# A gated recurrence and a soft mixture of experts on one Trainium2 core: seven experts' second layers summed in four row groups before one turn to 128 rows, and another order of the last partial sums

## The chip, the core and the metric

The kernel runs on one core of a Trainium2 chip. The metric is the device time of one execution in microseconds (us), and a kernel's figure is the median of several executions. The engines are TensorE (PE for its matmuls, PEld for its weight loads), VectorE (DVE), ScalarE (ACT), GpSimd (POOL) and SyncE (SP, which here only issues DMAs). Sixteen DMA engines move data between HBM and the core's SBUF; matmuls write to PSUM banks.

## What is computed

The input `x` is 4 batches x 5056 tokens x 256 channels. A gated recurrence runs over the tokens of each batch, and a soft mixture of experts follows on all 20224 rows of its output. Cut to what matters:

```python
f = lower_bound + (1 - lower_bound) * sigmoid(f_logit)
for t in range(S):
    h = f[:, t] * h + (1 - f[:, t]) * x[:, t]        # y[:, t] = h
logits = y @ phi                                     # 20224 x 32 slots (8 experts x 4)
d = softmax of logits over the rows                  # column by column
slot_input = d.T @ y                                 # 32 x 256
slot_out = per expert: relu(slot_input @ w1) @ w2    # w1 256 x 1024, w2 1024 x 256
out = (softmax of logits over the 32 slots) @ slot_out
```

The output is 20224 x 256 in float32.

## The kernel before, in words

The order of the instructions on every engine is the order of the code (a manual schedule): no planner moves them.

**Main loop (lines 479 to 566).** Forty units (10 token groups of 512 tokens x 4 batches) are loaded by SP, go through the sigmoid (ACT), the products (POOL), transposes (PE), the scan along the tokens (DVE), back to token order, and yield logits, their exponentials `etall` (slots on partitions, the four batches stacked as 4 x 32 = 128 rows) and the sum `slot_ps` of weighted rows. Meanwhile POOL issues the loads of the experts' weights (L135 to L147), w1 of all eight experts first, then w2. The tiles of the last two experts share one buffer, `w_t`; the last expert's tile comes in three parts of four, two and two of its eight chunks `fc`.

**Between loop and experts (L568 to L593).** POOL clears two tiles, `hid` (L571, 1024 columns of bf16) and `wide` (L572, 4096 columns). The last slot sums follow, and `spin` (L150) issues matmuls whose result nobody reads: six ahead of the copy of `slot_ps` (L584) and six behind the sum that makes the slot inputs (L593).

**The experts' first layer (L620 to L654).** For four experts at a time, `hi_ps` is computed in four strips of 32 output rows (L621); relu goes to `hi0` and `hi1`, and PE transposes them into `ht_ps`. Of a 32-column block only the expert's own four slots are wanted. For experts 0 to 3 they are copied into `hid` (L645, ACT), which is zero elsewhere, one 32-column block per expert and chunk. For experts 4 to 7 they are copied into `wide` (L653, twice ACT and twice DVE), repeated for the four batches, so a block has 128 columns.

**The second layer (L655 to L710).** This is where the change lies. Experts 0 to 3 use 128x32 matmuls: chunk `fc` goes to the row group `fc % 4` of the bank `so4_ps` (L658), so four matmuls can stand beside each other on the array, and the four row groups hold four partial sums of the 32 slots. DVE copies them to `so4` (L664), and one fp32 matmul with `rep2` (L719) adds the four groups and repeats the sum for the four batches: 128 rows, in the bank `so_ps`. Experts 4 to 7 use 128x128 matmuls (L705) that add the repeated rows directly to `so_ps`. Row sums of the exponentials (`row_sums`, L393) and four `spin` matmuls lie between the experts. The last expert's upper four chunks (`late`) go to another bank, `sb_ps`.

**The last sums (L688 to L736).** When the last expert's chunk 3 is summed, ACT makes `part_b` (L712, bf16) and DVE `part` (L713, fp32) from `so_ps`, both scaled. DVE's `slot_out` (L728) is `sb_ps` scaled plus `part`. For two rows of tokens the kernel goes around `slot_out`: `early_ps[r]` takes four matmuls with `gs`, which already holds the exponentials times the hidden values of the late chunks (`early_row`, L694), and one with `part_b` (`early_part`, L699). On PE the order is: late chunks 4 and 5, `early_row(0)` for them, `early_part(0)`, `early_part(1)`, late chunks 6 and 7, the other six of `early_row`. ACT scales both rows (L734, tile `early`) and SP stores each (L736). POOL makes `slot_bd` (L738, two instructions) from `slot_out`.

**The output stage (L741 to L845).** `pieces` (L774) makes the first block of the last batch: 32x256 matmuls from `slot_out` (`share`, L755) into PSUM banks `op`, evictions by DVE (L745) and ACT (L749) into two tiles `ob`, and a store by SP after every second or fourth row (L785). `couple` (L804) makes two batches at once from `slot_bd` (L811) into `oc`, stored at L817; `rest` (L834) and `whole` (L802) do what remains. The first two banks `op` are those that `early_ps` used.

Of the kernel before, what the change touches and what calls it, by code (L numbers as in the profile page):

```python
# [9 lines left out]
F32 = mybir.dt.float32  # L10
BF16 = mybir.dt.bfloat16
AX = mybir.AxisListType
ALU = mybir.AluOpType
ACT = mybir.ActivationFunctionType
# [4 lines left out]
def kernel(  # L19
# [10 lines left out]
    nc = tc.nc  # L30
    B, S, D = x.shape
    E = moe_w1.shape[0]
    F = moe_w1.shape[2]
    NS = moe_phi.shape[1]
    SPE = NS // E
    P = 128
    DC = D // P
    FC = F // P
    R = 4
    G = P * R  # L40
    n_grp = (S + G - 1) // G
# [18 lines left out]
    wide_r = 4 * R  # L60
# [60 lines left out]
    rrow = store.tile([P, n_grp * R, B], F32, name="rrow")  # L121
# [10 lines left out]
    w1_sb = [wts.tile([P, DC, F], BF16, name=f"w1_sb{e}") for e in range(E)]  # L132
    w2_sb = [wts.tile([P, FC, D], BF16, name=f"w2_sb{e}") for e in range(E - 2)]
# [16 lines left out]
    def spin(dst, k, w):  # L150
        for _ in range(k):
            nc.tensor.matmul(dst[:, ds(0, w)], w1_sb[0][:, 0, :P], w1_sb[0][:, 0, :w],
                             start=True, stop=True, skip_group_check=True)

    W_AT = {9: 1, 17: 1, 25: 1, 31: 1, 32: 1, 33: 2, 34: 3, 36: 6}
    w_next = [0]
# [4 lines left out]
    ld = held.enter_context(tc.tile_pool(name="ld", bufs=3))  # L161
    with tc.tile_pool(name="sp2", bufs=3) as sp2, \
# [316 lines left out]
        for n in range(n_unit):  # L479
# [82 lines left out]
            elif not n >= n_unit - 6:  # L562
# [2 lines left out]
                batch(slots, n - 4, 1)  # L565
                if n > 2 * B and n % (2 * B) == 3:
                    idle(1)
        hid, wide = (ld.tile([P, 2, R, D], F32, name=i, tag="x_t") for i in ("hid", "wide"))  # L568
        hid = hid.rearrange("p u r d -> p (u r d)").bitcast(BF16)[:, ds(0, FC * E // 2 * NS)]
        wide = wide.rearrange("p u r d -> p (u r d)").bitcast(BF16)[:, ds(0, FC * E // 2 * P)]  # L570
        nc.gpsimd.memset(hid, 0.0)  # L571
        nc.gpsimd.memset(wide, 0.0)  # L572
        hid = hid.rearrange("p (f e s) -> p f e s", f=FC, s=NS)
        wide = wide.rearrange("p (f w b s) -> p f w b s", f=FC, b=B, s=NS)
        logits(last, [3])
        late_exps()
        left_over()
# [3 lines left out]
        late_weights()  # L581
        slots(odd)
        late_slots()
        spin(tail[:, 1], 6, D)  # L584
        slot_sb = hpool.tile([P, G, DC], BF16, name="slot_sb", tag="h")
        slot_sb = slot_sb.rearrange("p t o -> p (t o)").bitcast(F32)[:, ds(0, D)]
        nc.vector.tensor_copy(slot_sb, slot_ps)
# [2 lines left out]
        for o in range(DC):  # L590
            nc.tensor.matmul(sin_ps[:, o], slot_v[:, o], rep[:, 0],
                             start=True, stop=True, skip_group_check=True)
        spin(slot_bank[:, 1], 6, D)  # L593

    with tc.tile_pool(name="ew", bufs=1) as ew, \
         tc.tile_pool(name="pm", bufs=2, space=PSUM) as pm, \
# [14 lines left out]
        Q = 4  # L611
# [20 lines left out]
        for q in range(E // Q):  # L632
            ht_ps = psu.tile([P, FC, P], BF16, name="ht_ps", tag="up")
            hi_v = his[q].rearrange("p (c f) -> p f c", f=FC)
            for fc in range(FC):
                nc.tensor.transpose(ht_ps[:, fc], hi_v[:, fc], ident)
            if q == 0:
                nc.tensor.matmul(cs_ps, rep2, cs1, start=True, stop=True)
                src = ht_ps.rearrange("p f (j s) -> p f j s", s=NS)[:, :, :, ds(0, SPE)]
                src = bass.AP(tensor=src.tensor, offset=src.offset,  # L640
                              ap=[list(src.ap[0]), [P, FC], [NS + SPE, Q], [1, SPE]])
                dst = hid[:, :, :, ds(0, SPE)]
                dst = bass.AP(tensor=dst.tensor, offset=dst.offset,
                              ap=[list(dst.ap[0]), [Q * NS, FC], [NS + SPE, Q], [1, SPE]])
                nc.scalar.copy(dst, src)  # L645
                nc.vector.reciprocal(rcs, cs_ps)
                nc.vector.tensor_tensor(of_last, of_last, rcs, ALU.mult)
                continue
            for j in range(Q):
                s0 = (Q + j) * SPE  # L650
                src = ht_ps[:, :, ds(j * NS + s0, SPE)]
                copy = nc.scalar.copy if j % 2 == 0 else nc.vector.tensor_copy
                copy(wide[:, :, j, :, ds(s0, SPE)],  # L653
                     src.unsqueeze(2).broadcast_to([P, FC, B, SPE]))  # L654
        so4_ps = pm.tile([P, D], F32, name="so4_ps", tag="pm")  # L655
        for e in range(Q):
            for fc in range(FC):
                nc.tensor.matmul(so4_ps[ds(fc % 4 * NS, NS), :], hid[:, fc, e],  # L658
                                 w2_sb[e][:, fc],
                                 start=(e == 0 and fc < 4),  # L660
                                 stop=(e == Q - 1 and fc >= FC - 4),
                                 skip_group_check=True)
        so4 = ew.tile([P, D], F32, name="so4")
        nc.vector.tensor_copy(so4, so4_ps)  # L664

        tail_b = ds((B - 1) * NS, NS)
        ex = ew.tile([P, 2, P], BF16, name="ex")
# [24 lines left out]
        def early_row(r, k, n):  # L692
            for i in range(k, k + n):
                nc.tensor.matmul(early_ps[r], gs[:, i, r], w2_sb[E - 1][:, FC - n_late + i],  # L694
                                 start=r == 0 and i == 0, stop=i == n_late - 1,
                                 skip_group_check=True)

        def early_part(r):
            nc.tensor.matmul(early_ps[r], e_only[:, r], part_b, start=r == 1, stop=False,  # L699
                             skip_group_check=True)  # L700

        for j in range(Q):
            for fc in range(FC):
                late = j == Q - 1 and fc >= FC - n_late
                nc.tensor.matmul(sb_ps if late else so_ps,  # L705
                                 wide[:, fc, j].rearrange("p b s -> p (b s)"),
                                 w2_sb[Q + j][:, fc],
                                 start=(j == 0 and fc == 0) or (late and fc == FC - n_late),
                                 stop=j == Q - 1 and fc in (FC - n_late - 1, FC - 1),
                                 skip_group_check=True)  # L710
                if j == Q - 1 and fc == FC - n_late - 1:
                    nc.scalar.activation(part_b, so_ps, ACT.Copy, scale=rcs)  # L712
                    nc.vector.tensor_scalar_mul(part, so_ps, rcs)  # L713
                if j == Q - 1 and fc == FC - 3:
                    early_row(0, 0, 2)
                    early_part(0)
                    early_part(1)
            if j == 0:
                nc.tensor.matmul(so_ps, rep2, so4, start=False, stop=False,  # L719
                                 skip_group_check=True)  # L720
                row_sums(1)
            if j == 1:
                row_sums(2)
                spin(unread, 4, D)
                q = n_grp * R - 1
                nc.vector.reciprocal(rrow[:, wide_r:q], rs_ps[:, wide_r:q])
                nc.vector.reciprocal(rrow[:, q, ds(0, B // 2)], rs_ps[:, q, ds(0, B // 2)])
        nc.vector.scalar_tensor_tensor(slot_out, sb_ps, rcs, part, ALU.mult, ALU.add)  # L728
        early_row(0, 2, 2)
        early_row(1, 0, 4)  # L730
        early = ew.tile([P, 2, D], F32, name="early")
        to_b = out[ds((B - 1) * S, P * wide_r)].rearrange("(p r) d -> p r d", r=wide_r)
        for r in range(2):
# [142 lines left out]
```

## Time and profile before

| what | us |
|---|---|
| median of 3 runs (lowest to highest) | 197.96 (197.57 to 198.35) |
| the profiled execution, its own time | 198.21 |
| its span, first to last instruction | 196.4 |
| PE / DVE / ACT / POOL busy | 149.9 / 144.1 / 142.6 / 103.3 |
| mean granted clock of TensorE | 0.866 |
| DMA moved | 70.75 MB |
| longest shares of the chain that ended last | DMA 37%, PE 25%, DVE 13% |

All positions are microseconds from the start of the span. A row of the timeline gives start, length, engine, line and the tile that is written and those that are read; in square brackets stands the idle time of the engine before it and what ended that. Consecutive instructions of one kind are drawn together with their count. The slices cut the span into 40 parts of 4.9 us; a digit is the busy share in tenths. A matmul's own length (0.27 us) is its way through the array; two of them start 0.109 us apart in steady flow, and that distance is what a further one costs.

### The profile page before, as it was taken

The numbers are of one execution on the slowest core, as the hardware profiler recorded it, in microseconds if no ns is written. First come the engines' busy times: TensorE is split into PE (matmuls) and PEld (weight loads), VectorE is DVE, ScalarE is ACT, GpSimd is POOL, SyncE is SP. The second block draws the span as 40 slices with busy tenths as digits, with TensorE's granted clock in tenths as the row PEclk, the third lists the DMA queues.
The fourth block names the chain that finished last, engine by engine and source line by source line (L and its number), as shares of the span: only waits on it lengthen the run. The fifth ranks groups of instructions, "written<-read, shape, count | busy, mean of one in ns | idle before, by whom it ended". The sixth has DMA issues, their size and how long they took to land.

```text
span 196.4 us, 3258 instructions
## 1 busy us (share of the span) xinstructions
PE 149.9 (76%) x1196; PEld 105.8 (54%) x1196; DVE 144.1 (73%) x185; ACT 142.6 (73%) x201; POOL 103.3 (53%) x78
## 2 busy tenths in 40 slices
PE   0687579789979979897998888999889999920000
PEld 0475458577766858665776766668664434300000
DVE  2669789998799999999999999343277988920000
ACT  3688778899699998999998797334089999950000
POOL 2689586894988588894969976291030000000000
PEclk9999999996999999999999999999995555555555
DMA  6999999999999999999999999999749999999994
GB/s 205 420 422 418 430 430 420 427 425 333 405 427 424 398 343 422 427 417 308 405 419 385 259 222 214 214 214 213 138 162 432 422 432 424 427 427 437 444 444 173
DMA packets 14161, 70.75 MB, mean 360 GB/s; under 512 B 1585, under 2 KB 2866, under 8 KB 10178
## 3 DMA queue, kind: packets, MB, share of 16 engines
q1 hardware_dynamic: 11520, 62.13, 76.5%
q0 software_dynamic: 2624, 8.42, 21.5%
q8 instruction: 9, 0.15, 0.3%
q14 instruction: 6, 0.05, 0.1%
q10 hardware_dynamic: 2, 0.00, 0.0%
HBM read 58.23 MB, written 20.71 MB: 402 GB/s over the span
## 4 chain that ended last, share of the span: by engine, by line
DMA 37%; PE 25%; DVE 13%; ACT 5%; POOL 4%; issue 4%; ACTq 0%; SPq 0%; POOLq 0%
DMA x_t<-in_x_dram 14%; DVE h L313 10%; PE op L811 8%; DMA w_t<-in_moe_w_dram 8%; DMA f_t<-in_f_logit_dram 7%; DMA w_sb<-in_moe_w_dram 7%; POOL u_t L246 4%; PE hp L326 4%; ACT oc L749 3%; PE up L267 3%; DVE ht L345 3%; PE sp L261 2%; PE op L755 2%; PE lg L359 1%; PE slot_ps L183 1%
## 5 line engine op out<-in xcount | busy, mean ns | idle before, releaser
L246 POOL TENSOR_TENSOR u_t<-s_t,x_t 128x1024 bf16<-128x1024 bf16 (+1 forms) x39 | 82.5, 2131 | 21.8 <-ACT s_t L235 12.3
L313 DVE TENSOR_TENSOR_SCAN h<-a,h,up 128x512 bf16<-128x512 f32 (+1 forms) x72 | 86.9, 1253 | 3.9 <-PE up L267 2.6
L235 ACT ACTIVATE s_t<-f_t 128x2048 bf16<-128x2048 f32 (+2 forms) x23 | 38.4, 1669 | 7.1 <-DMA f_t<-in_f_logit_dram 7.1
L326 PE MATMUL hp<-ident_f,h 128*128 128x128 f32 (+1 forms) x160 | 29.4, 308 | 8.0 <-DVE ht L345 5.8
L326 PEld LDWEIGHTS hp<-ident_f,h 128*128 128x128 f32 (+1 forms) x160 | 23.4, 207 | 18.7 <-DVE ht L345 10.9
L261 PE MATMUL sp<-ident_f,s_t 128*128 128x128 f32 x144 | 21.3, 291 | 6.8 <-ACT s_t L235 4.5
L295 ACT ACTIVATE a<-sp,lbs 128x1024 f32<-128x1024 bf16 x24 | 25.5, 1117 | 0.6 <-PE sp L261 0.6
L749 ACT ACTIVATE oc<-op,rrow 128x256 f32<-128x256 f32 x62 | 24.5, 508 | 0.2
L811 PE MATMUL op<-slot_bd,etall 64*128 64x512 bf16 x62 | 23.6, 594 | 0.4 <-POOL slot_bd L738 0.3
L261 PEld LDWEIGHTS sp<-ident_f,s_t 128*128 128x128 f32 x144 | 17.4, 150 | 8.7 <-ACT s_t L235 5.0
L745 DVE TENSOR_TENSOR oc<-op,rrow 128x512 f32<-128x512 f32 x31 | 20.0, 685 | 2.0 <-PE op L811 1.9
L302 ACT ACTIVATE a<-sp,lbs 128x512 f32<-128x512 bf16 (+2 forms) x22 | 17.8, 857 | 3.8 <-PE sp L261 3.5
L267 PE MATMUL up<-ident_f,u_t 64*128 64x64 f32 x192 | 17.6, 229 | 2.4 <-POOL u_t L246 2.4
L183 PE MATMUL slot_ps<-rep,ident_f 128*128 128x256 f32 x52 | 17.0, 422 | 1.0 <-POOL rep L86 1.0
L267 PEld LDWEIGHTS up<-ident_f,u_t 64*128 64x128 f32 x192 | 13.9, 138 | 6.3 <-POOL u_t L246 2.8
L811 PEld LDWEIGHTS <-etall 64*128 64x128 bf16 x62 | 9.2, 155 | 13.5 <-issue 7.8
L345 DVE COPY ht<-hp 128x512 f32<-128x512 f32 (+1 forms) x20 | 13.4, 670 | 1.4 <-PE hp L326 1.4
L345 ACT COPY ht<-hp 128x512 f32<-128x512 f32 (+1 forms) x20 | 11.7, 583 | 3.5 <-PE hp L326 3.4
L313 DVE TENSOR_TENSOR_SCAN h<-a,up 128x512 bf16<-128x512 f32 x8 | 9.3, 1207 | 2.5 <-PE up L261 2.5
L183 PEld LDWEIGHTS slot_ps<-rep,ident_f 128*128 128x128 f32 x52 | 8.3, 193 | 3.0 <-POOL rep L86 1.2
L359 PE MATMUL lg<-h,phi 128*32 128x512 bf16 (+1 forms) x80 | 9.4, 389 | 0.3 <-ACT et L383 0.2
L261 PE MATMUL up<-ident_f,u_t 128*128 128x128 f32 x48 | 8.9, 314 | 0.5 <-POOL u_t L246 0.5
(126 smaller groups left out, 150.3 us busy)
## 6 DMA issues: line engine op xcount, KB each, us to landing
f_t<-in_f_logit_dram SPq DMA_DIRECT2D x12, 1024.0 KB, 13.3
x_t<-in_x_dram SPq DMA_DIRECT2D x12, 1024.0 KB, 12.0
out_dram<-oc SPq DMA_DIRECT2D x6, 2048.0 KB, 13.7
w_sb<-in_moe_w_dram POOLq DMA_DIRECT2D x14, 512.0 KB, 11.1
f_t<-in_f_logit_dram SPq DMA_DIRECT2D x12, 512.0 KB, 8.4
x_t<-in_x_dram SPq DMA_DIRECT2D x12, 512.0 KB, 9.9
out_dram<-oc SPq DMA_DIRECT2D x4, 896.0 KB, 6.3
out_dram<-ob SPq DMA_DIRECT2D x1, 2048.0 KB, 9.8
```

The costliest lines, as they stand in the source:

```text
L183: nc.tensor.matmul(slot_bank[:, 1], ident_f, wide_rep, start=False, stop=False, skip_group_check=True)
L235: nc.scalar.activation(s_t, f_t, ACT.Sigmoid, scale=-1.0)
L246: nc.gpsimd.tensor_tensor(uts[n][:, :r], s_t[:, :r], x_t[:, :r], ALU.mult)
L261: nc.tensor.transpose(ps[:, :, r], t[:, r], ident_f)
L267: nc.tensor.transpose(v[:, :, r], t(r)[k].bitcast(F32), ident_f[k, k])
L295: nc.scalar.activation(a, sp[:, :, :, :, o], ACT.Identity, scale=nomlb[:, ds(o, 1)], bias=1.0)
L313: nc.vector.tensor_tensor_scan(h[:, :T, o], decays[n // 2, o][:, n % 2, :T], up[:, :T, o], hs[number(g - 1, b)][:, ds(used(g - 1) - 1, 1), ...
L326: nc.tensor.transpose(hp[:n_p, r], hw[:, :n_p, r], ident_f)
L345: copy(hts[g][:n_p, b].rearrange("p r d -> p (r d)").bitcast(F32), hps.pop(n)[:n_p].rearrange("p r c -> p (r c)"))
L745: nc.vector.tensor_tensor(ob, op, scale.broadcast_to(list(ob.shape)), ALU.mult)
L749: nc.scalar.activation(ob[:, i], op[:, i], ACT.Copy, scale=scale[:, i])
L811: nc.tensor.matmul(op.rearrange("p u d -> p (u d)"), ew[:, :, r], slot_bd[ds(j * 2 * NS, 2 * NS)].rearrange("s u d -> s (u d)"), start=Tru ...
```

## The change

The second layer of experts 4 to 6 is done as that of experts 0 to 3 was: narrow matmuls in four row groups, into one bank `sum_ps` for all seven. After expert 6, DVE copies the bank to `total`, and the fp32 matmul with `rep2` opens `so_ps`; only the last expert adds 128 wide rows to it. `hid` and `wide` now share one tile, with 1792 and 1024 columns. The copy of the second transposed half takes one ACT copy (experts 4 to 6) and one DVE copy (expert 7) instead of four. Each block of six dummy matmuls becomes two, and 16 narrow ones (`narrow`); between the experts stand four, six and four in place of one block of four. DVE makes `part` first, from `so_ps`, and ACT makes `part_b` from `part`. On PE, the direct rows' first two chunks of both rows now stand ahead of the late chunks 6 and 7, and `early_part` is the last matmul of each row.

```diff
+    def narrow(dst, k):
+        for i in range(k):
+            nc.tensor.matmul(dst[ds(i % B * NS, NS), ds(0, D)], w1_sb[0][:, 0, ds(0, NS)],
+                             w1_sb[0][:, 0, ds(0, D)], start=True, stop=True,
+                             skip_group_check=True)
...
-        hid, wide = (ld.tile([P, 2, R, D], F32, name=i, tag="x_t") for i in ("hid", "wide"))
-        hid = hid.rearrange("p u r d -> p (u r d)").bitcast(BF16)[:, ds(0, FC * E // 2 * NS)]
-        wide = wide.rearrange("p u r d -> p (u r d)").bitcast(BF16)[:, ds(0, FC * E // 2 * P)]
+        hid = ld.tile([P, 2, R, D], F32, name="hid", tag="x_t")
+        hid = hid.rearrange("p u r d -> p (u r d)").bitcast(BF16)
+        n_hid, n_wide = FC * (E - 1) * NS, FC * P
+        wide = hid[:, ds(n_hid, n_wide)]
+        hid = hid[:, ds(0, n_hid)]
         nc.gpsimd.memset(hid, 0.0)
         nc.gpsimd.memset(wide, 0.0)
         hid = hid.rearrange("p (f e s) -> p f e s", f=FC, s=NS)
-        wide = wide.rearrange("p (f w b s) -> p f w b s", f=FC, b=B, s=NS)
+        wide = wide.rearrange("p (f b s) -> p f b s", f=FC, s=NS)
...
-        spin(tail[:, 1], 6, D)
+        spin(tail[:, 1], 2, D)
+        narrow(tail[:, 1], 16)
...
-        spin(slot_bank[:, 1], 6, D)
+        spin(slot_bank[:, 1], 2, D)
+        narrow(slot_bank[:, 1], 16)
...
+            k = Q if q == 0 else Q - 1
+            s0 = q * Q * SPE
+            src = ht_ps[:, :, ds(s0, SPE)]
+            src = bass.AP(tensor=src.tensor, offset=src.offset,
+                          ap=[list(src.ap[0]), [P, FC], [NS + SPE, k], [1, SPE]])
+            dst = hid[:, :, q * Q, ds(s0, SPE)]
+            dst = bass.AP(tensor=dst.tensor, offset=dst.offset,
+                          ap=[list(dst.ap[0]), [(E - 1) * NS, FC], [NS + SPE, k], [1, SPE]])
+            nc.scalar.copy(dst, src)
+            if q == 0:
                 nc.vector.reciprocal(rcs, cs_ps)
                 nc.vector.tensor_tensor(of_last, of_last, rcs, ALU.mult)
                 continue
-            for j in range(Q):
-                s0 = (Q + j) * SPE
-                src = ht_ps[:, :, ds(j * NS + s0, SPE)]
-                copy = nc.scalar.copy if j % 2 == 0 else nc.vector.tensor_copy
-                copy(wide[:, :, j, :, ds(s0, SPE)],
-                     src.unsqueeze(2).broadcast_to([P, FC, B, SPE]))
-        so4_ps = pm.tile([P, D], F32, name="so4_ps", tag="pm")
-        for e in range(Q):
+            s0 = (E - 1) * SPE
+            src = ht_ps[:, :, ds((Q - 1) * NS + s0, SPE)]
+            nc.vector.tensor_copy(wide[:, :, :, ds(s0, SPE)],
+                                  src.unsqueeze(2).broadcast_to([P, FC, B, SPE]))
+        sum_ps = pm.tile([P, D], F32, name="sum_ps", tag="pm")
+
+        def expert(e):
             for fc in range(FC):
-                nc.tensor.matmul(so4_ps[ds(fc % 4 * NS, NS), :], hid[:, fc, e],
+                nc.tensor.matmul(sum_ps[ds(fc % 4 * NS, NS), :], hid[:, fc, e],
                                  w2_sb[e][:, fc],
                                  start=(e == 0 and fc < 4),
-                                 stop=(e == Q - 1 and fc >= FC - 4),
+                                 stop=(e == E - 2 and fc >= FC - 4),
                                  skip_group_check=True)
-        so4 = ew.tile([P, D], F32, name="so4")
-        nc.vector.tensor_copy(so4, so4_ps)
+
+        for e in range(Q):
+            expert(e)
 
...
-                                 start=r == 0 and i == 0, stop=i == n_late - 1,
-                                 skip_group_check=True)
+                                 start=i == 0, stop=False, skip_group_check=True)
 
         def early_part(r):
-            nc.tensor.matmul(early_ps[r], e_only[:, r], part_b, start=r == 1, stop=False,
+            nc.tensor.matmul(early_ps[r], e_only[:, r], part_b, start=False, stop=True,
                              skip_group_check=True)
 
-        for j in range(Q):
-            for fc in range(FC):
-                late = j == Q - 1 and fc >= FC - n_late
-                nc.tensor.matmul(sb_ps if late else so_ps,
-                                 wide[:, fc, j].rearrange("p b s -> p (b s)"),
-                                 w2_sb[Q + j][:, fc],
-                                 start=(j == 0 and fc == 0) or (late and fc == FC - n_late),
-                                 stop=j == Q - 1 and fc in (FC - n_late - 1, FC - 1),
-                                 skip_group_check=True)
-                if j == Q - 1 and fc == FC - n_late - 1:
-                    nc.scalar.activation(part_b, so_ps, ACT.Copy, scale=rcs)
-                    nc.vector.tensor_scalar_mul(part, so_ps, rcs)
-                if j == Q - 1 and fc == FC - 3:
-                    early_row(0, 0, 2)
-                    early_part(0)
-                    early_part(1)
-            if j == 0:
-                nc.tensor.matmul(so_ps, rep2, so4, start=False, stop=False,
-                                 skip_group_check=True)
-                row_sums(1)
-            if j == 1:
-                row_sums(2)
-                spin(unread, 4, D)
-                q = n_grp * R - 1
-                nc.vector.reciprocal(rrow[:, wide_r:q], rs_ps[:, wide_r:q])
-                nc.vector.reciprocal(rrow[:, q, ds(0, B // 2)], rs_ps[:, q, ds(0, B // 2)])
+        expert(Q)
+        row_sums(1)
+        spin(unread, 4, D)
+        expert(Q + 1)
+        row_sums(2)
+        spin(unread, 6, D)
+        q = n_grp * R - 1
+        nc.vector.reciprocal(rrow[:, wide_r:q], rs_ps[:, wide_r:q])
+        nc.vector.reciprocal(rrow[:, q, ds(0, B // 2)], rs_ps[:, q, ds(0, B // 2)])
+        expert(Q + 2)
+        total = ew.tile([P, D], F32, name="total")
+        nc.vector.tensor_copy(total, sum_ps)
+        spin(unread, 4, D)
+        nc.tensor.matmul(so_ps, rep2, total, start=True, stop=False, skip_group_check=True)
+        for fc in range(FC):
+            late = fc >= FC - n_late
+            nc.tensor.matmul(sb_ps if late else so_ps,
+                             wide[:, fc].rearrange("p b s -> p (b s)"),
+                             w2_sb[E - 1][:, fc],
+                             start=fc == FC - n_late,
+                             stop=fc in (FC - n_late - 1, FC - 1),
+                             skip_group_check=True)
+            if fc == FC - n_late - 1:
+                nc.vector.tensor_scalar_mul(part, so_ps, rcs)
+                nc.scalar.copy(part_b, part)
+            if fc == FC - 3:
+                early_row(0, 0, 2)
+                early_row(1, 0, 2)
         nc.vector.scalar_tensor_tensor(slot_out, sb_ps, rcs, part, ALU.mult, ALU.add)
-        early_row(0, 2, 2)
-        early_row(1, 0, 4)
+        for r in range(2):
+            early_row(r, 2, 2)
+            early_part(r)
```

More of the change, by code (lines that the diff above doesn't have):

```diff
@@ L638 @@
                 nc.tensor.matmul(cs_ps, rep2, cs1, start=True, stop=True)
[L639 to L645, printed above, removed]
+            k = Q if q == 0 else Q - 1
[8 more added lines that the diff above has]
+            if q == 0:
                 nc.vector.reciprocal(rcs, cs_ps)
```

## The prediction

> **What bounds the kernel now.** I read the page's 40 slices first, then the stretches of the last 55 us, the chain of waits, SP's queue, and the timeline of 139 to 146 us. The slices say that the DMA engines are the bound almost everywhere, with one hole:
>
> ```profile
> DMA  6999999999999999999999999999749999999994
> ...
> GB/s 205 420 422 418 430 430 420 427 425 333 405 427 424 398 343 422 427 417 308 405 419 385 259 222 214 214 214 213 138 162 432 422 432 424 427 427 437 444 444 173
> ```
>
> To 142 us the loads fill them, from about 146 to 193.5 the stores do, and in between (slices 28 and 29) lies the only time that computation can win or lose. The stretches show the hole's edges; columns are busy us and count for PE, PEld, DVE, ACT and POOL, then clock, DMA share and GB/s:
>
> ```profile
> 142.00:143.50 1.50, 1.27 (x12) 0.87 (x9) 0.97 (x2) 0.62 (x2) 0.00 (x0) 1.00 0.00 0
> ...
> 144.75:145.50 0.75, 0.51 (x5) 0.40 (x4) 0.75 (x2) 0.75 (x3) 0.72 (x1) 1.00 0.06 10
> 145.50:146.25 0.75, 0.73 (x4) 0.47 (x4) 0.75 (x2) 0.75 (x3) 0.00 (x0) 1.00 0.75 259
> 146.25:150.00 3.75, 3.65 (x14) 1.28 (x12) 3.75 (x8) 3.75 (x12) 0.00 (x0) 0.64 1.05 417
> ```
>
> From 145.50 the store queue holds work until the end, so the end moves as the first `ob` store moves. What leads to it:
>
> ```profile
> 125.11 16.37 DMA w_t<-in_moe_w_dram
> ...
> 142.97 0.49 DVE slot_out L728
> 143.47 0.05 issue
> 143.51 0.67 PE op L755 x4
> ```
>
> ```profile
> 142.01 0.48 DVE L713 TENSOR_SCALAR part<-so_ps,rcs 128x256 f32<-128x256 f32 x1 [2.64 <-ACT part_b L712]
> 142.02 0.38 PE L699 MATMUL early_ps<-part_b,e_only 128*128 128x256 bf16 x2
> ...
> 142.88 0.91 ACT L734 ACTIVATE early<-early_ps,rrow 128x256 f32<-128x256 f32 x2 [0.90 <-PE early_ps L694]
> ```
>
> ```profile
> 143.41 1.67 SPq L736 DMA_DIRECT2D out_dram<-early  x2
> 145.18 2.37 SPq L785 DMA_DIRECT2D out_dram<-ob  x5
> ```
>
> The w2 tiles land late (expert 6 at 139.51, the last expert's three parts at 140.76, 141.47 and 142.10, by their semaphores); then `part`, `slot_out`, the first output matmul at 143.51. But the chain leaves out SP. The first two-row piece of `ob` is evicted by 144.68 (DVE, 143.99 + 0.69), and its store issues at 145.18 only: SP sends the second `early` store from 143.86 and is held in it for 1.23 us, to 145.09. So the end hangs on **ACT early (142.88), its two stores, SP's 1.23 us, the first `ob` store**; `slot_out` ends in an eviction that has 0.5 us to spare.
>
> **The change, part by part.**
>
> *Ahead of 139.5.* Each spin block of six wide matmuls becomes two wide and four waves of four narrow ones. The 32 narrow matmuls of L658 took 1.06 us, eight wide of L705 1.03 us: 0.13 and 0.129 for a wave of four or one wide, so a block costs the same. Each change of shape costs 0.1 us more (last L455 at 126.25, next wide L152 at 126.46: 0.21 for 0.11). Experts 4 and 5 cost the same in waves of eight matmuls over two (0.22 each in steady flow against 8 x 0.109 = 0.87), less by 0.65 each. Spins 4, 6 and 4 in place of 4 add 10 x 0.11 = 1.1. The memsets shrink (128x4096 took 3.53, 128x1024 0.97; 1792 + 1024 columns make 2.6 for 4.5), one wide copy on each of ACT and DVE goes (0.27, 0.23). The fp32 `so4` sum (L719, 0.43 to the next) moves behind expert 6. All of it is hidden by the landing of expert 6: PE idled 0.53 us before 139.56 and the spins are there to fill. Uncovered it would cost its own length, at most 0.3 us.
>
> [...]
>
> *139.5 to 142.* Expert 6 now takes two waves: 139.56 to the last start at 139.67, less the eight starts to 140.32 of before. Then a new serial step: `total`, DVE, from PSUM. Its row is L664 (so4, 128x256 f32, 0.415), and PE's end to DVE's start is 0.31 to 0.34 (as 141.13 to 141.42 for `part_b`'s semaphore): 139.67 + 0.34 + 0.42 = 140.43, + 0.11 to PE, fp32 matmul 140.55 + 0.43, first wide matmul of expert 7 at 140.98. Before, part 1 let it start at 140.80. Four of them: the last starts at 141.31 against 141.13. **+0.18**, still ahead of part 2 (141.47), so fc 4 and 5 stay at 141.52 and 141.63. Without a landing in front the new step would show in full, 0.87 us more.
>
> *Partial sum.* Before, ACT read `so_ps` first (141.50, 0.47), DVE after it (142.01, 0.48) and `part` ended 142.49. Now DVE reads first: 141.31 + 0.31 = 141.62, + 0.48 = 142.10. **-0.39** for `part`. `part_b` becomes ACT's copy of `part`, SBUF to bf16, which no row shows: from 0.27 (L645, 128x128 from PSUM) to 0.59 (L345, 128x512 f32); I take 0.42, near L712's 0.47 for the same size. So `part_b` is ready at 142.12 + 0.42 = 142.54 (142.39 to 142.71), where it was 141.97: **+0.57**. That wait is PE's: behind it stand early_part(0), early_row(1) and early_part(1), but the sums `sb` no longer stand behind it.
>
> *PE.* fc 4 and 5, four direct rows (141.74 to 142.07), fc 6 at 142.17 (part 3 lands 142.10) and fc 7 at 142.28; before 142.24 and 142.35: **-0.07**. `slot_out` starts when both are there. Before, it started 0.48 after `part` ended and 0.34 after the sum; DVE's next instruction after a plain wait starts within 0.05 elsewhere, so it was `part`'s own tail. Now: max(142.10 + 0.48, 142.28 + 0.31) = 142.59 for 142.97, **-0.38**.
>
> *Direct rows.* early_row(0) goes at 142.39 and 142.50, early_part(0) at max(142.61, 142.54 + 0.05) = 142.61, early_row(1) at 142.72 and 142.83, early_part(1) 142.94. ACT's first `early` follows by 0.31: 142.92 for 142.88; the second after it (0.47): 143.40 for 143.35. **+0.04**; with `part_b` at 142.71 it is +0.2, and with 142.39 it is unchanged, as PE gets there at 142.61.
>
> *Output stage.* Its first matmul waits for `slot_out` (143.08 now) and for ACT's first `early` (a shared PSUM bank; 143.42 for 143.36): 143.45 for 143.51, -0.06. `slot_bd` on POOL is 0.38 earlier, but the first matmul that it feeds (145.52, waited 0.26 for it) makes `oc` stores (first at 148.92), which queue behind most of 2 MB of `ob`. SP: same order of stores; both `early` stores 0.04 later, hence the held SP free at 145.13 and the first `ob` store at 145.23. Nothing else is issued in between. POOL's queue and the loads on SP are in the same order as before.
>
> **The sum.** End +0.04, taken as +0.05. The profiled execution is 198.21 us (span 196.4 and 1.8 around it), so 198.26; its own distance to the median 197.96 of three runs (197.57 to 198.35) is +0.25. **198.0 us** beside that median. The slot path's 0.38 us is real, I think, and buys nothing.
>
> **Rivals.** A difference under 0.5% (1.0 us) is about what a measurement of this kernel can't tell from none.
>
> *A, slower: the clock is gated in the hole.* The granted clock falls to 0.50 in 44.92 to 48.34 and from 147.32 on:
>
> ```profile
> 41.51:44.92 3.41, 2.45 (x30) 1.93 (x31) 3.22 (x5) 3.39 (x5) 2.87 (x3) 1.00 1.00 418
> 44.92:48.34 3.42, 3.42 (x27) 2.63 (x27) 3.42 (x4) 2.98 (x3) 1.16 (x1) 0.50 1.04 329
> 55.16:58.58 3.42, 2.42 (x17) 1.78 (x18) 3.40 (x4) 3.42 (x4) 2.73 (x2) 1.00 1.00 419
> 143.91:147.32 3.41, 3.05 (x22) 2.10 (x21) 3.33 (x6) 3.12 (x9) 1.56 (x2) 1.00 0.63 225
> ```
>
> Busy time does not tell it: 2.45 and 3.05 were followed by it, 2.42 was not. Columns streamed, weighted by the rows and columns of the array in use, do. In 143.91 to 147.32 stand 9 matmuls of L811 (512 columns, half of the array) and 13 of L755 (256 columns, a quarter), 3,136 full columns of the 8,000 that a window holds at 256 in 0.109 us: 0.39, or 0.36 with those at the edges cut there. So counted (fp32 doubled) both windows before a throttle have 0.36, every other one 0.41 or more. My count for the changed kernel is 0.43 at its lowest between 136.6 and 140. If it falls under the point between 0.36 and 0.41, PE runs at half speed for 3.4 us about 140 to 143: the last expert's matmuls and the rows, about 14 starts after the last landing at 0.22 for 0.11, +1.2 to +1.9: 199.2 to 199.9.
>
> [...]
>
> *B, slower, small: the last landing moves.* PE fetches instructions through the same DMA engines (16 KB, about 0.6 us of one engine, at 124.35, 134.63 and 143.74). With 68 more PE instructions the last comes 68 earlier, at 139 to 142. If on the engine that brings part 3 last, +0.1 to +0.6: 198.1 to 198.6. Also here: the narrow matmuls don't overlap as L658's did (0.87 for 0.22): +0.65 on `part`, +0.5 at the end.
>
> *C, faster: SP's hold goes.* The 1.23 us may be a collision with that fetch at 143.74, or grow less with other timing. The store then follows the eviction, 144.62 for 145.18: up to -0.5, 197.4. Against: 1.2 us shows on the second store after each idle stretch, as at L802 (1.18).
>
> *D, faster: the end hangs on `slot_out` or `slot_bd` after all*: -0.38, 197.6, or 0.6 with C's part, to 197.0.
>
> *E: it doesn't do as it says*: the order on PE is written by hand, so I give this nothing of its own.
>
> **How the numbers follow.** Forecast 0.56; A 0.11; B 0.13; C 0.1; D 0.1. Forecast and most of B, C and D lie within 0.5%. Faster by more needs C with D: 0.08. Slower by more: A, and a tail of B: 0.14. Same: 0.78. The range runs from 197.2 (C and D in part) to 199.0 (B, and the mild end of A).
>
> **What would show it.** Right: expert 7's first matmul near 140.98, `part` without a wait for ACT at 141.6, `slot_out` near 142.6, ACT `early` still near 142.9, first `ob` store near 145.2. Wrong: a clock of 0.50 between 139 and 143; `early` before 142.7 or after 143.1; a second `early` store that does not hold SP; an end that moves by 0.38 with `slot_out` though the first `ob` store stands still.

## The result, and the profile after

The changed kernel takes 198.86 us (median of 20 runs, 197.67 to 199.08), the kernel before 198.05 in the same series (20 runs, 197.57 to 198.40). The ratio is 1.0028 with a 95% interval of 1.0019 to 1.0038: slower by 0.3%, within the half per cent that the forecast called no change, but clear of noise. The times fall into two groups: six spans of 195.9 to 196.4 us and fourteen of 196.8 to 197.3. The profiled execution (198.09 us, span 196.3) belongs to the first; run a_again below caught the second (198.93, span 197.2).

The slices of the page, DMA and GB/s, look as before, with the hole in slices 28 and 29:

```profile
DMA  5999999999999999999999999999749999999994
GB/s 205 417 422 417 434 429 421 427 427 385 350 426 427 422 310 427 424 417 351 361 422 417 241 213 214 215 213 215 144 158 431 422 432 424 427 427 437 437 451 177
```

The stretches of the hole (columns as before):

```profile
142.00:143.50 1.50, 1.50 (x16) 1.25 (x13) 0.83 (x2) 0.43 (x2) 0.00 (x0) 1.00 0.00 0
...
144.75:145.50 0.75, 0.75 (x9) 0.69 (x7) 0.75 (x2) 0.75 (x3) 0.75 (x1) 1.00 0.72 238
145.50:146.25 0.75, 0.73 (x5) 0.47 (x4) 0.75 (x3) 0.75 (x3) 0.15 (x1) 1.00 0.72 259
146.25:150.00 3.75, 3.53 (x14) 1.51 (x13) 3.75 (x8) 3.75 (x12) 0.00 (x0) 0.63 1.05 416
```

The timeline of the changed kernel, from expert 6 to the first `ob` store:

```profile
140.08 0.40 PE L670 MATMUL sum_ps<-w_t,hid 128*32 128x256 bf16 x8
...
142.19 0.48 DVE L737 TENSOR_SCALAR part<-so_ps,rcs 128x256 f32<-128x256 f32 x1 [1.23 <-PE so_ps L730]
...
142.71 0.40 ACT L738 CAST part_b<-part 128x256 bf16<-128x256 f32 x1 [5.13 <-DVE part L737]
...
143.16 0.49 DVE L742 SCALAR_TENSOR_TENSOR slot_out<-sb_ps,rcs,part 128x256 bf16<-128x256 f32 x1 [0.48 <-PE sb_ps L730]
...
143.47 0.84 ACT L749 ACTIVATE early<-early_ps,rrow 128x256 f32<-128x256 f32 x2 [0.36 <-PE early_ps L711]
...
144.01 0.82 SPq L751 DMA_DIRECT2D out_dram<-early  x2
...
145.13 1.31 SPq L800 DMA_DIRECT2D out_dram<-ob  x3
```

Two things differ from the forecast. PE reaches expert 6 at 140.08 without having waited, though its data had landed at 139.30: in this execution the clock was at 0.50 in 24.3 to 31.2 and 48.2 to 51.6, and the main loop ended 1.9 us later than in the profile of before (L461 at 127.82, there L455 at 125.91). That the clock made it late is not shown: a_less26 below had 0.50 in 21.8 to 28.7 and in 45.7 to 49.1, as long, and its loop ended 1.2 us earlier than this one. So `early` comes at 143.47 for 142.88. And SP's two `early` stores take 0.82 together where they took 1.67: the hold of 1.23 us in the second is gone, and the first `ob` store issues at 145.13 for 145.18. A loss of 0.6 and a gain of 0.8 hide each other; the 0.2 left over goes into a wait of the `ob` store for its eviction (to 145.10).

In a_again, of the second group, the same rows read so:

```profile
139.67 0.40 PE L670 MATMUL sum_ps<-w_t,hid 128*32 128x256 bf16 x8 [0.81 <-DMA w_t<-in_moe_w_dram]
...
141.14 0.60 PE L730 MATMUL so_ps<-w_t,hid 128*128 128x256 bf16 x4
142.90 0.39 PE L730 MATMUL sb_ps<-w_t,hid 128*128 128x256 bf16 x2 [1.17 <-DMA w_t<-in_moe_w_dram]
```

```profile
144.85 0.82 SPq L751 DMA_DIRECT2D out_dram<-early  x2
145.97 1.31 SPq L800 DMA_DIRECT2D out_dram<-ob  x3
```

Here PE has time to spare ahead of expert 6 (0.81 idle), as forecast, and then waits 1.17 us for the last expert's second part. By their semaphores its second and third part landed at 142.86 and 143.20, where the profile of before has 141.47 and 142.10. In the trace each load raises its semaphore sixteen times, read here as once by each DMA engine: fifteen had delivered by 141.59 and 142.22, and one was about a microsecond behind (1.27 and 0.98). SP is not held here either. The first `ob` store is 0.79 later than before, and the span 0.7 longer (197.2 for 196.4).

What moved is a packet of queue q8, which the DMA part of a trace calls `instruction`: nine packets of 16 KB in the profile of before and nine in that of the changed kernel, 0.88 to 0.97 us each, called fetches here. That they go with PE's instructions is read from the runs: b_pad34 and b_pad8 add matmuls, with their weight loads, and nothing else, and the last packet began at 141.73 and 142.48 there. It began at 143.74 in the kernel before, between loads and stores. The change adds 34 matmuls and 34 weight loads on PE, and the packet began at 140.77 in a_again and at 141.51 in the profiled execution, where one engine had just sent its last packet of w2 (141.49 to 141.51). A packet does not name its engine in the trace, so that the fetch ran on that one is inferred from the times. The DMA view of 140.75 to 142.75 us (40 slices of 0.05 us) of a_again has the fetch in its first slice and packets of w2 to the end; that of the kernel before, shown at b_pad34, has none behind 141.8:

```profile
DMA  9537345325241641521440202020101011011011
...
q8 instruction: 1, 0.02, 3.0%
```

### The profile page after: what moved, and what is told of

The parts are those of the page before. It is cut to its first block, busy times and chain, and to the rows that moved or that the text cites. A ratio compares the mean times of both kernels' runs of the same rounds, so it can differ in the third digit from the quotient of the medians.

```text
span 196.3 us, 3323 instructions
## 1 busy us (share of the span) xinstructions
PE 151.8 (77%) x1230; PEld 106.1 (54%) x1230; DVE 144.0 (73%) x184; ACT 142.1 (72%) x200; POOL 101.2 (52%) x78
## 4 chain that ended last, share of the span: by engine, by line
PE 42%; DVE 23%; ACT 10%; DMA 8%; issue 4%; POOL 1%; SPq 0%; ACTq 0%; POOLq 0%
DVE h L319 18%; PE op L826 9%; DMA f_t<-in_f_logit_dram 8%; PE hp L332 6%; PE sp L267 4%; DVE ht L351 4%; ACT oc L764 3%; PE up L273 3%; PE op L770 3%; ACT a L308 3%; PE lg L365 2%; PE slot_ps L189 2%; ACT s_t L241 2%; PE tail L399 1%; PE slot_ps L416 1%
## 5 line engine op out<-in xcount | busy, mean ns | idle before, releaser
L332 PE MATMUL hp<-ident_f,h 128*128 128x128 f32 (+1 forms) x160 | 30.0, 313 | 8.2 <-DVE ht L351 6.8
L267 PE MATMUL sp<-ident_f,s_t 128*128 128x128 f32 x144 | 21.9, 296 | 6.7 <-ACT s_t L241 4.5
L189 PE MATMUL slot_ps<-rep,ident_f 128*128 128x256 f32 x52 | 17.5, 432 | 0.8 <-POOL rep L86 0.8
L267 PE MATMUL up<-ident_f,u_t 128*128 128x128 f32 x48 | 9.4, 326 | 0.6 <-POOL u_t L252 0.5
```

Source lines behind the costliest of these rows:

```text
L189: nc.tensor.matmul(slot_bank[:, 1], ident_f, wide_rep, start=False, stop=False, skip_group_check=True)
L267: nc.tensor.transpose(ps[:, :, r], t[:, r], ident_f)
L332: nc.tensor.transpose(hp[:n_p, r], hw[:, :n_p, r], ident_f)
```

## The experiments

Three theories. **Fetch:** the added PE instructions pull the last fetch into the landing of w2 and out of SP's way; the sums have little part in it. **Sum** (with its forms cover and order): the new sums, dummies or order cost the time by themselves. **Hold:** SP's 1.23 us were worth what they showed. The clock was a fourth. All ratios are to the kernel before.

| kernel | median, us | ratio (95%) | last fetch at | part 3 lands | second `early` store, us | first `ob` store |
|---|---|---|---|---|---|---|
| before | 198.05 | | 143.74 | 142.10 | 1.23 | 145.18 |
| changed | 198.86 | 1.0028 (1.0019 to 1.0038) | 141.51 | 142.00 | 0.38 | 145.13 |
| a_again | 198.81 | 1.0024 (1.0005 to 1.0043) | 140.77 | 143.20 | 0.38 | 145.97 |
| a_spins | 198.49 | 1.0021 (1.0008 to 1.0034) | 143.82 | 142.30 | 1.09 | 145.34 |
| b_order | 198.14 | 1.0005 (0.9994 to 1.0016) | 143.48 | 142.13 | 0.87 | 144.90 |
| b_merge | 197.28 | 0.9958 (0.9944 to 0.9972) | 143.69 | 142.09 | none | 144.69 |
| b_pad34 | 198.84 | 1.0047 (1.0030 to 1.0065) | 141.73 | 143.73 | 0.38 | 146.06 |
| a_pad94 | 199.56 | 1.0089 (1.0064 to 1.0114) | 144.85 | 143.16 | 1.16 | 146.26 |
| a_merge | 198.36 | 1.0021 (1.0009 to 1.0034) | 141.50 | 143.53 | none | 145.97 |
| a_spins_merge | 197.44 | 0.9977 (0.9962 to 0.9991) | 143.72 | 142.19 | none | 144.71 |
| b_pad8 | 197.83 | 0.9989 (0.9967 to 1.0011) | 142.48 | 142.03 | 0.60 | 144.65 |
| a_less26 | 197.68 | 0.9971 (0.9950 to 0.9993) | 142.36 | 141.98 | 0.38 | 144.47 |
| b_order_merge | 197.78 | 0.9973 (0.9951 to 0.9995) | 144.42 | 142.18 | none | 145.02 |
| a_less26_merge | 197.19 | 0.9970 (0.9958 to 0.9982) | 142.57 | 142.10 | none | 144.63 |

The last four columns are each kernel's one profiled execution.

**a_again**, the changed kernel unaltered.

> The changed kernel once more, to have a second trace of it: its times fall into two groups, spans of 195.9 to 196.4 us and of 196.8 to 197.3 us. Hold theory: the groups differ in SP being held in its second `early` store or not; a trace with a span near 197.1 shows that store with 1.2 us and the first `ob` store near 145.8, one near 196.3 shows 0.4 us and 145.1. Clock theory: a span near 197.1 shows a granted clock of 0.50 somewhere between 128 and 145 us, and SP's store as short as in the other.

The trace in the group of 197 shows neither: SP is not held, and the clock is 1.00 from 128 to 145 us. It showed the late part and the fetch, and so the fetch theory was formed here.

**a_spins**, the old dummies in the changed kernel:

```diff
-        spin(tail[:, 1], 2, D)
-        narrow(tail[:, 1], 16)
+        spin(tail[:, 1], 6, D)
...
-        spin(unread, 4, D)
...
-        spin(unread, 6, D)
+        spin(unread, 4, D)
```

> The changed kernel with the dummy matmuls of the kernel before (six wide, six wide, four wide; no narrow ones, none behind experts 4 and 6). Cover theory (PE's work ahead of expert 6 is no longer hidden by its landing, 139.30 against PE at 140.08, and everything behind it is 0.5 to 0.6 us late): PE waits for the landing again, ACT's first `early` goes from 143.47 to about 142.9, and the time from 198.86 to about 198.1. Order theory (the direct rows are late because `part_b` and the two matmuls that use it now come last): ACT's `early` stays near 143.4 and the time near 198.8. Clock theory: with fewer dummies the clock falls to 0.50 between 128 and 143 us, 199 or more.

198.49: between the two. `early` is at 143.17, and w2 lands 0.2 us later than in the profile of before (expert 6 at 139.75). The clock stays at 1.00 from 15.2 to 148.3 us without the new dummies, which ends the clock theory. These 34 matmuls less also move the fetch back to 143.82, so this run does not tell cover from fetch; the next ones do. With the fetch in its old place it is still 0.2% slower than the kernel before, clear of noise. In its trace `early` comes 3.38 us after expert 6 starts, as forecast (3.36); the rest is the later landing and 0.3 more in the stage of stores (51.5 us from the first `ob` store to the end, 51.3 before), and no run shows whether the sums cause either.

**b_order**, the kernel before with only the change's order:

```diff
-                    nc.scalar.activation(part_b, so_ps, ACT.Copy, scale=rcs)
                     nc.vector.tensor_scalar_mul(part, so_ps, rcs)
+                    nc.scalar.copy(part_b, part)
...
-                    early_part(0)
-                    early_part(1)
+                    early_row(1, 0, 2)
```

> The kernel before with only the last part of the change: `part` first, `part_b` from `part`, and the matmuls of `part_b` last in each direct row. Cover theory: `part` about 0.4 us earlier, `slot_out` at about 142.6, ACT's first `early` within 0.1 us of 142.88, time 198.0 to 198.2. Order theory: ACT's first `early` 0.4 to 0.6 us later, time 198.5 to 198.9. That the end hangs on `slot_out`: 197.6.

198.14, no difference. `slot_out` starts at 142.63 (142.97 before), `early` at 142.96 (142.88):

```profile
141.46 0.48 DVE L711 TENSOR_SCALAR part<-so_ps,rcs 128x256 f32<-128x256 f32 x1 [1.74 <-PE so_ps L704]
...
142.63 0.48 DVE L726 SCALAR_TENSOR_TENSOR slot_out<-sb_ps,rcs,part 128x256 bf16<-128x256 f32 x1 [0.69 <-PE sb_ps L704]
...
142.96 0.84 ACT L733 ACTIVATE early<-early_ps,rrow 128x256 f32<-128x256 f32 x2 [0.58 <-PE early_ps L698]
...
143.48 0.92 PE L754 MATMUL op<-slot_out,etall 32*128 32x256 bf16 x7 [0.23 <-ACT early L733]
```

The last row shows why 0.34 us of `slot_out` buy nothing: the first output matmul now waits for ACT's `early` instead.

**b_merge**, one store for both `early` rows:

```diff
-            nc.sync.dma_start(out=to_b[:, ds(r, 1)], in_=early[:, ds(r, 1)])
+        nc.sync.dma_start(out=to_b[:, ds(0, 2)], in_=early)
```

> The kernel before with one store for both `early` rows, issued when both are there, in place of two. Hold theory (SP is held 1.23 us in its second store, and the first `ob` store waits for SP alone): no second store to be held in, the first `ob` store at 144.7 in place of 145.18, time about 197.6. If the hold moves to the next store, or the first `ob` store waits for its eviction: 198.0 to 198.1.

197.28. The first `ob` store goes to 144.69, where its eviction ends:

```profile
143.83 0.35 SPq L736 DMA_DIRECT2D out_dram<-early  x1
144.69 2.62 SPq L785 DMA_DIRECT2D out_dram<-ob  x5
```

That is 0.49 of the 0.9 us by which the span falls (195.5 for 196.4). The rest lies in the stage of stores: from the first `ob` store to the end of the span 51.2 to 51.3 us pass in before, changed, a_again, b_pad34 and a_less26, and 50.8 to 50.9 in four of the five kernels with one store (in the fifth, b_order_merge, that `ob` store was itself held). No run shows why.

**b_pad34**, the kernel before with 34 small dummy matmuls in the units 12 to 28 (they write, with `start=True`, beside the slot sums in the same PSUM bank, and what it stores is not the function's output):

```diff
+                if 12 <= n < 29:
+                    for i in range(2):
+                        nc.tensor.matmul(slot_bank[ds(i % B * NS, NS), 1, ds(0, 4)],
+                                         ident[:, ds(0, NS)], ident[:, ds(0, 4)],
+                                         start=True, stop=True, skip_group_check=True)
```

> The kernel before with 34 small dummy matmuls more (32 columns of weights, 4 columns of data, two in each of the units 12 to 28, where the loads bound the kernel), as many PE instructions as the change adds; nothing else differs. Fetch theory (what costs is that PE's last 16 KB instruction fetch, 143.74 before, comes so many instructions earlier, among the loads of the last expert, and sets one DMA engine about 1 us back): the fetch goes to 139 to 142 us, the last parts of w2 land 1 us later in most runs, the hold of SP in the second `early` store goes, and the time goes to about 198.5 (143.2 for the last part, 142.9 + 1.1 for ACT's `early`, + 1.66 to the first `ob` store, 145.6 for 145.18), in two groups. Where the fetch misses the last parts: about 197.4 to 197.6, as only the hold is gone. Sum theory (the new sums and dummies cost it by themselves): 198.05 as before.

198.84, in one group of six runs: at least the whole loss of the change, without one edit of it. The DMA view of 140.75 to 142.75 us (40 slices of 0.05 us), first of the kernel before, then of this one:

```profile
DMA  7776676645644132011000000000000000000000
...
q0 software_dynamic: 86, 0.07, 23.0%
```

```profile
DMA  6666745672532320110900000000000000000000
...
q0 software_dynamic: 76, 0.06, 20.2%
q8 instruction: 1, 0.02, 3.0%
```

The slice with a 9 is the fetch, counted where it starts (141.73; it took 0.97). A load of weights has sixteen packets of 4 bytes in the trace (304 for 19 loads in the kernel before), read here as one by each engine, its last of the load. Of those that end w2, fifteen had gone by 141.57; the sixteenth stands at 142.69 to 142.71, at the end of the fetch (142.70). The semaphore came at 143.73, and PE waited:

```profile
142.34 0.38 PE L704 MATMUL early_ps<-part_b,e_only 128*128 128x256 bf16 x2 [0.19 <-ACT part_b L717]
143.77 0.38 PE L710 MATMUL sb_ps<-w_t,wide 128*128 128x256 bf16 x2 [1.05 <-DMA w_t<-in_moe_w_dram]
```

This execution, too, had a late main loop (expert 6 at 140.25, landed at 139.46), but the wait of 1.05 us shows that the landing of part 3 came last.

**a_pad94**, the same dummies in the changed kernel, 94 of them, 128 with those of the change (output as in b_pad34):

```diff
+                if 12 <= n < 36:
+                    for i in range(4 if n < 35 else 2):
```

> The changed kernel with 94 small dummy matmuls more in the units 12 to 35: with the 34 that the change adds they make 128, about one fetch of 16 KB, so the fetches fall where they fell in the kernel before. Fetch theory: the last fetch near 143.7 again, the last part of w2 at 142.0 to 142.3, SP held about 1.1 us in the second `early` store, one group of times, about 198.1 to 198.5. Sum theory: 198.8 in two groups, as the changed kernel.

The last fetch is behind the loads again (144.85) and SP is held again (1.16), as the theory said, but the time is 199.56. This trace has ten such fetches, the others nine. So the ninth, the last one of the changed kernel (141.51), now comes at 137.05, and one engine is 1.1 us late in all landings behind it: expert 6 at 140.60 (139.51 before), part 3 at 143.16. So this kernel pays for both. The expectation had looked at the last fetch only.

**a_merge**, the edit of b_merge in the changed kernel:

> The changed kernel with one store for both `early` rows, which made the kernel before 0.8 us faster. Fetch theory: here SP is not held in the second store, since the fetch that meets it came earlier; so nothing is gained, 198.7 to 198.9, and the last parts still land late in most runs. That two stores cost their 0.8 us anywhere: 198.0.

198.36, below the 198.7 to 198.9 expected; the ratio is 1.0021 beside 1.0024 and 1.0028 with two stores: no gain clear of the intervals, and not the 0.8 us of the other theory. The fetch comes ahead of the end of w2 (141.50), part 3 is late (143.53) and the first `ob` store is where it was in a_again (145.97), so there was no hold to take away. Its span is 0.3 shorter (196.9 for 197.2), the store stage's share seen at b_merge.

**a_spins_merge**, the edits of a_spins and of b_merge together:

> The changed kernel with the dummies of the kernel before (last fetch at 143.8, behind the loads) and one store for both `early` rows. Neither the fetch nor the hold is in it, so beside the kernel before with one store (197.28) it shows what the new sums and the new order cost alone. By the prediction's sum 0.05: 197.3. By the run with the old dummies, 0.4: 197.7.

197.44, above b_merge by 0.16 in the medians and 0.4 by the ratios, whose intervals overlap. So by this pair the sums and the order alone cost between nothing and 0.4 us; the forecast's 0.05 lies in it. b_merge has 5 runs only.

**b_pad8**, eight dummies more in the kernel before (they add to a region nobody reads):

```diff
+                if 12 <= n < 16:
+                    for i in range(2):
...
+                                         start=False, stop=False, skip_group_check=True)
```

> The kernel before with only 8 small dummy matmuls more (units 12 to 15), which compute nothing that is used. Fetch theory: PE's last 16 KB fetch moves from 143.74 to about 142.3 to 142.9, behind the last completion packet of w2 (141.8) and ending before SP's second `early` store is issued (143.86); no engine is late, SP is not held (0.4 us in place of 1.23), the first `ob` store follows its eviction at 144.7, time about 197.4: eight instructions more make the kernel 0.6 us faster. If the hold belongs to the second of two small stores and not to the fetch: 198.05, as before.

The trace is close to what was expected: fetch at 142.48, part 3 at 142.03, the second `early` store 0.60 for 1.23 (0.4 was expected), the first `ob` store at 144.65. The time, 197.83, is not clear of no change. In this execution that `ob` store was itself held, 0.68 for 0.39, while an 8 KB packet of another queue ran (144.44 to 145.19). So where the fetch goes is confirmed, and the gain is not.

**a_less26**, the changed kernel with 26 dummies fewer:

```diff
-        narrow(tail[:, 1], 16)
+        narrow(tail[:, 1], 3)
...
-        narrow(slot_bank[:, 1], 16)
+        narrow(slot_bank[:, 1], 3)
```

> The changed kernel with 26 of its dummies taken out (each block of 16 narrow ones becomes three), sums, order and both `early` stores as they are. Fetch theory: the net count is 8 matmuls over the kernel before, so the last fetch falls behind the loads and ahead of the stores, at about 142.5; the last parts of w2 land at 142.0 to 142.3, no hold, ACT's first `early` near 142.9 to 143.0, time 197.4 to 197.6 in one group: the change would then have been a gain of 0.5. Sum theory (sums, `total` and order cost the time): 198.6 to 198.9. Clock theory: the clock at 0.50 in 128 to 143 us, over 199.

197.68, one group (spans 195.7 to 196.3), a gain of 0.3% on the kernel before in the same series (197.98). The sums and the order are those of the change. The view of the same 2 us shows the fetch alone, behind the loads, and SP goes through:

```profile
DMA  5765845645236130100000000000000090000000
```

```profile
143.35 0.82 SPq L751 DMA_DIRECT2D out_dram<-early  x2
144.47 2.62 SPq L800 DMA_DIRECT2D out_dram<-ob  x5
```

The dummies taken out also give PE more time ahead of expert 6 (0.77 us idle), but a_again had 0.81 and was slow all the same. And b_pad8, in the same series, is the kernel before with as many PE instructions and the fetch in the same place (142.48): 197.83 there, 197.68 here, with intervals that overlap. With the fetch out of the way in both, the new sums and order show no cost clear of noise.

**b_order_merge**, the edits of b_order and of b_merge together:

> The kernel before with one `early` store and the change's order of partial sum and direct rows. Prediction's working: `slot_out` 0.35 us earlier, but the first output matmul waits for ACT's first `early`, which stays within 0.1 us, so 197.2 to 197.4 as with one store alone (197.28). That the order had a gain which only SP's hold hid: 196.9 to 197.0.

197.78 (197.15 to 198.35), above the 197.2 to 197.4 expected. Inconclusive: the profiled execution is one whose main loop ran late (PE at expert 6 at 140.57 after its landing at 139.59), so nothing of the expected rows could be read. It shows that the cover ahead of expert 6 is thin in the kernel before too. And it shows a hold with a single `early` store: the fetch ran from 144.42 to 145.42, and the first `ob` store, issued at 145.02, took 0.77, to 0.37 behind the fetch's end. So the hold does not belong to the second `early` store as such.

**a_less26_merge**, the edits of a_less26 and of b_merge together:

> The changed kernel with 26 dummies fewer (last fetch between loads and stores) and one store for both `early` rows. Fetch theory: both effects away, the first `ob` store at its eviction, about 144.5, and a little less in the store stage, as with one store in the kernel before: 197.1 to 197.4, below both kernels. If one store only helped by taking the hold away, which is not there in this one: 197.7, as with the 26 fewer alone.

197.19, as the fetch theory had it and below both kernels; with b_merge (197.28, 5 runs) the fastest measured.

## Why the prediction was right and wrong

The measured time lies in the range, and the change of 0.3% is within what the forecast called none, but the true sum has other terms than the forecast's 0.05. That 198.86 lies in the range is luck in part: rival B, which came true, was sized at 198.1 to 198.6, and the range reached 199.0 for the mild end of rival A, which did not occur.

*What bounds.* Right: the end follows the first `ob` store. From it to the end of the span are 50.8 to 51.5 us in every profile.

*Ahead of 139.5, hidden.* Right where the loop is in time (PE idle 0.81 before expert 6 in a_again, 0.77 in a_less26), wrong in the profiled execution, whose late loop used the cover up. The forecast took one execution's 0.53 us of idle as given.

*139.5 to `early`.* Right. From expert 6's start to the first wide matmul of the last expert 1.42 were forecast and 1.47 measured (a_less26, 139.42 to 140.89); to `part` 2.06 and 2.11; to `slot_out` 3.03 and 3.07; to `early` 3.36 and 3.39. With a landing 0.14 earlier, `early` is at 142.81 for a forecast of 142.92. `part_b` took 0.41 (0.42 taken). That `slot_out` buys nothing (rival D) is shown by b_order.

*The clock (rival A).* Did not occur: the granted clock is 1.00 from 51.6 to 147.2, also with the fewer dummies of a_spins.

*The fetch (rival B).* Named, with the right time for the fetch (139 to 142), but it failed in size and in chance. "+0.1 to +0.6" on the last landing at a small chance; it was +1.1 (a_again, and +1.4 on the second part, for which PE waited) and +1.4 (a_merge), and 1.6 in b_pad34, where the fetch met part 3 too, and the slower group, of which a_again is one, holds fourteen of twenty runs. The upper end was the fetch's own length on one engine, and that was an estimate which no row shows: "about 0.6 us" is what 16 KB take at a sixteenth of the 427 GB/s of a full slice, and the three packets in the trace of before took 0.94 to 0.96. Nor did the forecast see that the last 4 bytes of a load can stand behind the packet too (1.1 us behind the other fifteen in b_pad34), and that the semaphore comes later still (1.0 us after the 4 bytes in b_pad34, 0.3 in the kernel before).

*SP's hold (rival C).* Named with its cause and given 0.1; the hold is gone in both traces of the changed kernel, with the fetch. In the four profiles with a hold of 0.87 us or more in that store its end stands 0.36 to 0.39 us behind the fetch's end (145.09 behind 144.70 before; a_spins, b_order and a_pad94 alike). The argument against, that the same 1.2 us shows at L802, compared it with a store that waits in a full store stage, where no fetch runs.

B and C are one event: the fetch left the place where it held SP for 0.85 us, worth 0.5 at the first `ob` store (b_merge), and took one where it set the last two parts of w2 back by 1.4 and 1.1. Forecasting them as separate rivals, with separate small chances, was the error. In a_again `early` comes 1.43 later (144.31 for 142.88), the two stores take 0.85 less (0.82 for 1.67), and the `ob` store then waits 0.21 more for its eviction (145.25 + 0.69): 0.79 in all, as measured. With one `early` store, and so no hold in either kernel, the late landing shows in full: the first `ob` store comes 1.28 later (145.97 in a_merge, 144.69 in b_merge).

Which engine the fetch meets matters as much as when. The engines do not end a load together: in the last thirteen loads of the experts' weights in the kernel before, the first raise of the semaphore comes 1.8 to 1.9 us ahead of the last. By the sixteen raises of each load, the fetch of 134.63 there met an engine that was about 1.5 us ahead of the last and still was 0.6 ahead afterwards (load of 137.09), so it delayed nothing. In a_again, b_pad34, a_merge and a_pad94 the fetch that did harm met one of those within about 0.1 us of the last: in all four the ninth of the execution, where that of 134.63 is the eighth.

Open: what decides the engine of a fetch; what in SP waits for the fetch; and how far the late loop, and how far the fetch just missing the last packet, makes the faster group of the changed kernel.

## What to carry to other kernels

In this long unrolled kernel nine fetches of 16 KB stand in the DMA trace among the packets of the tensors, and adding or removing a few matmuls ahead of them moved the later ones (eight were enough to move the last one from 143.74 to 142.48). Before costing an edit, look up in the DMA part of the trace when the instruction queue's packets start, count how far the edit shifts them, and see what lands or is stored there, and whether the engine that they meet is one of the last; move them to a gap with the number of dummies before judging the edit itself. Where a kernel's times fall into two groups, take a trace of each.

## What the runs showed that was not expected

A fetch of 16 KB (0.95 us on one of sixteen engines) made a 128 KB load land up to 1.6 us later (143.73 for 142.10), and held the issue of a 128 KB store for 1.23 us where it takes 0.38 without. Moving one such packet, with 26 dummy matmuls fewer, was worth 0.6% of the whole time between the changed kernel and a_less26 (198.86 and 197.68, each beside its own series of the kernel before: 1.0028 and 0.9971). And one store of two rows in place of two single ones took 0.3 to 0.4 us from the end beyond what the hold explains.
